# A planner of instruction order gets margins for the later expert searches, and ScalarE copies every expert's transposed tokens

## The chip, the core and the metric

The kernel runs on one core of a Trainium2 chip. TensorE (PE) multiplies matrices, VectorE (DVE), ScalarE (ACT) and GpSimd (POOL) work element by element, SyncE (SP) issues transfers, and DMA engines move data between the chip's memory and the core's two on-chip buffers, SBUF and PSUM; PE writes to PSUM only. The metric is the time of one execution on the device in microseconds (us), as the median of several runs; lower is better.

## The reference

Three parts follow one another: an attention whose keys and values are means over 8 rows, a mixture of experts in which each of 8 experts takes exactly as many tokens as its capacity, and a second MLP.

```python
scores = scale * np.matmul(q, k_p.transpose(0, 1, 3, 2))   # B=8, H=8, S=576, D=64; k_p, v_p pooled by 8
out    = softmax(scores) @ v_p                             # -> x: 4608 tokens x 512

logits = x @ w_gate                                        # 4608 x 8
cap    = N // E                                            # 576
order  = np.argsort(-logits.flatten())
for idx in order:                                          # the largest logits first
    tok, e = idx // E, idx % E
    if assigned[tok] >= 0 or counts[e] >= cap:
        continue
    assigned[tok] = e
    counts[e] += 1
for e in range(E):
    mask = assigned == e
    out[mask] = np.maximum(x[mask] @ w1[e], 0.0) @ w2[e]   # 512 -> 1024 -> 512

h = out @ w_in                                             # 512 -> 2048
y = (h - np.tanh(h)) @ w_out                               # 2048 -> 512
```

## The kernel before

After the attention the tokens' logits lie on chip and the tokens x in a buffer in the chip's memory (xd). `moe1` (L1190) then goes over the experts in the order in which they fill up. For step k it routes (`route`, L831, and `route_rows`, L920), writes down the work of the expert before (`expert(k - 1)`, L1140), and gathers the tokens of step k (`gather`, L1089).

A route finds the expert that fills next and the logit at which it is full. For k of 1 to 6 that is a search (`search`, L754) in steps: DVE compares logits with a row of thresholds (tile at), PE counts by 36 products with a one-hot matrix (rt<-at,ohb), DVE compares the counts with the places that are free (pass), PE spreads that over the partitions (rt<-pass,ones), and DVE picks the next thresholds. `fill` (L849) then marks the expert's tokens (sel), ranks them with a product on PE (`ahead`, L900: rt<-sel and rt<-run), makes their places (`slots`, L910) and takes the expert out of the logits. `route_rows` turns places into a list of row numbers: one-hot tables oa (DVE) and ob (DVE and POOL), 36 products of them (tr<-ob,oa), a cast (sp), five products (tr<-sp), and at last the numbers ix. `gather` fetches 5 tiles of token rows (xg) by an indirect transfer on POOL (L1098), transposes each with four PE instructions into the one PSUM tile of the name tr, and makes two parts of it: xh, a rounded copy (ACT), and xl, the rest (DVE). Every large matrix is held in two such parts, and a product of two matrices is three products of parts. All these parts are called "parts" in the trace. For expert 1 alone ACT first copies the PSUM tile over the row tile xg, which isn't needed any more, and both parts are taken from that copy.

`expert` does the first layer (8 tiles of 24 matmuls of 288 columns, into m and mm), splits its result in two (ACT, then DVE), and `outputs` (L1172) does the second. The weights come by SP's queue in tiles wr; ACT and DVE split them in two. Beside this, with low urgency, the weights of the second MLP are converted (tiles raw, ca, cd, cm, on DVE, ACT and POOL) and stored by SP's queue. `second_mlp` (L1236) begins when these and the first tiles of y, loaded by SP, are split.

The order of all this isn't the order of the code. `Plan` (L101) records every instruction with its reads and writes (so all of them carry line 129 in the profile), and `placed` (L228) takes the instructions whose inputs are placed by their urgency, the smaller number first, and puts each into the earliest gap on its engine. Between an instruction and one that uses its result it counts a fixed time (`latency`, L221). One unit of urgency is an eighth of an expert. Route k has 8k − 12.5, the gather 8k − 4.6, the first layer of expert k 8k to 8k + 3, its second 8k + 4 to 8k + 7. What comes out is a fixed order for each engine, in which an engine that waits for one instruction holds back all behind it.

Of the kernel before, what the change touches and what calls it, by code (L numbers as in the profile page):

```python
# [50 lines left out]
class Ring:  # L51


    def __init__(self, pool, banks=False):
        self.pool, self.banks, self.tiles, self.next = pool, banks, {}, {}
# [45 lines left out]
class Plan:  # L101
# [9 lines left out]
    def __init__(self, nc):  # L111
        self.nc = nc
        self.ops, self.seen = [], {}
        self.busy, self.done = {}, 0
        self.urgency = 0.0
        self.tensor, self.vector, self.scalar, self.gpsimd, self.sync = [
            Recorder(self, n) for n in ("tensor", "vector", "scalar", "gpsimd", "sync")]

# [47 lines left out]
    def call(self, engine, fn, ins, outs, cost, delay=0.0):  # L166

        op = self.Op()
        op.engine, op.fn, op.cost, op.delay, op.transfer = engine, fn, cost, delay, 0.0
        op.urgency, op.index, op.deps, op.users, op.end = self.urgency, len(self.ops), {}, [], None  # L170
        for aps, write in ((ins, False), (outs, True)):
            for ap in aps:
                name, lo, hi, p, q, dense = self.region(ap)
                log = self.seen.setdefault(name, [])
                keep = []
                for e in log:
                    o, w, lo2, hi2, p2, q2 = e
                    hit = lo < hi2 and lo2 < hi and p < q2 and p2 < q
                    if o is not op and hit and (write or w):
                        op.deps[o] = op.deps.get(o, False) or w  # L180
                    if not (write and dense and lo <= lo2 and hi2 <= hi and p <= p2 and q2 <= q):
                        keep.append(e)
                keep.append((op, write, lo, hi, p, q))
                self.seen[name] = keep
        for o in op.deps:
            o.users.append(op)
        self.ops.append(op)
        return op

    def after(self, op, other):  # L190
        if other not in op.deps:
            op.deps[other] = True
            other.users.append(op)
# [27 lines left out]
    def latency(self, op, user):  # L221
        if user.engine == op.engine and not op.transfer:
            return op.delay + (0.0 if op.engine == "tensor" or not user.deps[op] else 0.127)
        if user.engine == "tensor":
            return op.delay + (0.25 if op.engine == "scalar" else 0.22)
        return op.delay + (0.2 if op.engine == "tensor" or op.transfer else 0.14)

    def placed(self):  # L228
# [48 lines left out]
class Kernel:  # L277
# [571 lines left out]
    def fill(self, k, hl, t1, t2, ws, fl, after):  # L849

        c, rp, mw, L = self.c, self.rp, self.mw, self.L
        V = self.plan.vector
        more, at, gt = [rp.tile([128, NT], F32, name=nm) for nm in ("e1", "e2", "gt")]
        V.scalar_tensor_tensor(at, hl[:, 0], t1, mw, op0=OP.is_equal, op1=OP.mult)
        V.scalar_tensor_tensor(more, hl[:, 0], t1, mw, op0=OP.is_gt, op1=OP.mult)
        V.tensor_tensor(more, more, self.aid, op=OP.add)
        V.tensor_reduce(ws, fl, axis=AX.X, op=OP.max)
        V.scalar_tensor_tensor(gt, hl[:, 1], t2, at, op0=OP.is_gt, op1=OP.mult)
        V.scalar_tensor_tensor(at, hl[:, 1], t2, at, op0=OP.is_equal, op1=OP.mult)
        V.tensor_tensor(self.aid, more, gt, op=OP.add)  # L860
        sel = rp.tile([128, 2 * NT], BF, name="sel")
        V.tensor_scalar(sel[:, NT:], at, ws, None, op0=OP.is_equal)
        V.tensor_scalar(sel[:, :NT], self.aid, ws, None, op0=OP.is_equal)
        p1 = self.ahead(sel)
        val = rp.tile([128, 2 * NT], F32, name="val")
        V.scalar_tensor_tensor(val, p1, CAP - 0.5, sel, op0=OP.is_lt, op1=OP.mult)
        g = self.slots(k, p1, val)

        self.plan.urgency += 4.0
        cl = rp.tile([128, 8], F32, name="cl")  # L870
        V.tensor_scalar(cl, c["w8"], ws, -4.0e37, op0=OP.is_equal, op1=OP.mult)
        V.tensor_scalar(cl, cl, 1.0e37, None, op0=OP.add)
        ei = rp.tile([1, 1], I32, name=f"ei{k}")
        V.tensor_scalar(ei, ws[:1], -1.0, 8.0, op0=OP.mult, op1=OP.add)
        self.ei[k] = ei
        V.tensor_tensor(L, L, cl[:, None, :].to_broadcast([128, NT, 8]), op=OP.min)
        V.scalar_tensor_tensor(self.open, self.open, ws, self.open, op0=OP.not_equal, op1=OP.mult)
        after()
        if 0 < k < E - 2:
            self.best()  # L880
        V.scalar_tensor_tensor(self.aid, val[:, NT:], ws, self.aid, op0=OP.mult, op1=OP.add)
        self.plan.urgency -= 4.0
        return g

    def rest(self, live):
# [203 lines left out]
    def gather(self, k):  # L1089

        nc, P = self.nc, self.plan
        P.urgency = 8 * k - 4.6 if k else -12.5
        xh, xl = [self.fp.tile([128, 4, CAP], F32R, name=nm) for nm in ("xh", "xl")]
        rows = []
        for i in range(5):
            n = 64 if (k % 2 == 0 and i == 4) else 128
            xg = self.cv.tile([128, DM], F32, name="xg", bufs=5)
            op = P.call("gpsimd", lambda xg=xg, n=n, i=i: nc.gpsimd.indirect_dma_start(  # L1098
                out=xg[:n], out_offset=None, in_=self.xd,
                in_offset=bass.IndirectOffsetOnAxis(ap=self.idx[k][:n, i:i + 1], axis=0)),  # L1100
                [self.idx[k][:n, i:i + 1]], [xg[:n]], 1.3 if k == 0 else 1.04, 2.3 if k > 2 else 2.0)
            op.transfer = n * DM * 4 / 360e3
            self.gathered = op
            rows.append((xg, n))
        col = 0
        for i, (xg, n) in enumerate(rows):
            p0 = 64 if (k % 2 == 1 and i == 0) else 0
            if k or i % 3 == 0:
                pt = self.mps.tile([128, 4, 128], F32, name="tr")
            else:  # L1110
                pt = self.mps.tile([128, 2, 512], F32, name="mm", bufs=2)[:, 0].rearrange("p (d n) -> p d n", d=4)
            for d in range(4):
                P.tensor.transpose(pt[:, d, :n], xg[:n, d * 128:(d + 1) * 128], self.c["ident"][:n, :n])
            cs = slice(col, col + n - p0)
            if k == 1:

                xf = xg[:, :4 * n].rearrange("p (d n) -> p d n", d=4)
                P.scalar.activation(xf, pt[:, :, :n], AF.Copy)
                pt = xf
            P.scalar.activation(xh[:, :, cs], pt[:, :, p0:n], AF.Copy)  # L1120
            P.vector.tensor_tensor(xl[:, :, cs], pt[:, :, p0:n], xh[:, :, cs].bitcast(F32), op=OP.subtract)
            col += n - p0
        return xh, xl
# [66 lines left out]
    def moe1(self):  # L1190
        P = self.plan
        self.ei, self.ev, self.turns = {}, {}, 0
        for k in range(E):
            P.urgency = 8 * k - 12.5
            g = self.route(k)
            self.route_rows(k, g)
            if k:
                self.expert(k - 1)
            self.x = self.gather(k)
        self.expert(E - 1)  # L1200


# [256 lines left out]
```

## Time and profile before

| | us |
|---|---|
| median of 3 runs | 1507.74 |
| lowest and highest of them | 1506.91, 1509.02 |
| the profiled execution | 1509.08 |
| its span, from the first to the last instruction | 1507.3 |

The profiled execution lies 1.34 us above the median. In its span PE is busy 1445.5 us (96%), DVE 1194.8 (79%), ACT 796.2 (53%) and POOL 311.5 (21%). The attention ends and the first routing begins at about 148 us; the experts run from about 192 to 700 us, the second MLP until the end. A row of a timeline gives the start, the duration, the engine, the operation with what it writes and reads, and in brackets how long the engine had been idle and for what. A duration of "x24" is that of the whole row.

### The profile page before, as it was taken

The page shows a single profiled execution, that of the slowest core. Times are in us where ns is not written, and L with a number is a line of the kernel's source. Part 1 is how long each engine was busy: PE and PEld are TensorE (multiplying, and loading weights), DVE is VectorE, ACT ScalarE, POOL GpSimd, SP SyncE. Part 2 cuts the span into 40 slices and gives each one's busy share as a digit, 9 for nine tenths or more (in the row PEclk, how much of TensorE's full clock was granted, in tenths as well). Part 3 has the DMA queues.
Part 4 walks back from the last instruction along what each step waited for, and adds up shares of the span by engine and source line. Part 5 has one row for each costly group of instructions (what it writes and reads, how often), then busy time and mean ns, then how long its engine had stood idle before and what let it go on. Part 6 is the DMA issues. An engine that isn't in the chain of part 4 may idle for free.

```text
span 1507.3 us, 25587 instructions
## 1 busy us (share of the span) xinstructions
PE 1445.5 (96%) x9763; PEld 1272.5 (84%) x9764; DVE 1194.8 (79%) x2506; ACT 796.2 (53%) x1433; POOL 311.5 (21%) x292
## 2 busy tenths in 40 slices
PE   8999579999999998999999999999999999999997
PEld 7999368999998998999778888888888888888885
DVE  8777877767888887975998787877878787877874
ACT  5444114334463546884666565656556555565653
POOL 5873201102133225552411000010101001010101
PEclk9999689999999999999999999999999999999999
DMA  9942114424253456775201010000101000000000
GB/s 386 379 157 78 61 35 127 126 81 154 76 179 103 142 173 207 229 249 168 88 15 56 1 49 8 29 29 15 42 0 50 7 29 28 28 29 1 28 1 28
DMA packets 98315, 138.51 MB, mean 92 GB/s; under 512 B 6928, under 2 KB 70416, under 8 KB 95504
## 3 DMA queue, kind: packets, MB, share of 16 engines
q1 hardware_dynamic: 87632, 108.04, 21.1%
q0 software_dynamic: 5952, 19.40, 3.7%
q10 hardware_dynamic: 4608, 9.44, 1.6%
q8 instruction: 76, 1.25, 0.3%
q14 instruction: 47, 0.39, 0.1%
HBM read 103.30 MB, written 33.55 MB: 91 GB/s over the span
## 4 chain that ended last, share of the span: by engine, by line
PE 77%; DVE 16%; DMA 3%; issue 2%; ACT 1%; POOL 1%; SPq 0%; POOLq 0%; ACTq 0%; DVEq 0%
PE mm L129 36%; PE m L129 17%; PE tr L129 7%; PE rt L129 7%; PE av L129 4%; DVE parts L129 3%; PE sc L129 3%; PE pt L129 2%; DVE g L129 2%; DVE ca L129 2%; PE rt L659 1%; DVE oa L129 1%; DVE at L129 1%; DVE ob L129 1%; DMA wr<-w 1%
## 5 line engine op out<-in xcount | busy, mean ns | idle before, releaser
L129 PE MATMUL mm<-parts 128*128 128x288 f32 x2112 | 307.3, 300 | 3.8 <-DVE parts L129 3.8
L129 PEld LDWEIGHTS mm<-parts 128*128 128x128 f32 x2112 | 288.2, 190 | 7.1 <-DVE parts L129 3.9
L129 PE MATMUL mm<-parts,gh 128*128 128x512 f32 x792 | 243.9, 389 | 0.0
L129 DVE SCALAR_TENSOR_TENSOR g<-s,g 128x512 f32<-128x512 f32 x288 | 205.9, 715 | 2.8
L129 ACT ACTIVATE s<-u,pb 128x512 f32<-128x512 f32 x288 | 192.5, 724 | 0.0
L129 PEld LDWEIGHTS mm<-parts,gh 128*128 128x128 f32 x792 | 148.7, 188 | 30.9
L129 PE MATMUL mm<-parts,gl 128*128 128x512 f32 x396 | 154.4, 390 | 1.7 <-DVE gl L129 1.7
L1308 POOL DMA_INDIRECT out<-y,ix x18 | 20.1, 1116 | 657.8 <-ACT y L129 637.4
L129 PE MATMUL m<-parts 128*128 128x288 f32 x960 | 144.1, 301 | 0.0
L129 PE MATMUL m<-yh,parts 128*128 128x512 f32 x432 | 141.7, 389 | 0.0
L129 ACT ACTIVATE parts<-wr 128x512 fp32r<-128x512 f32 x148 | 90.5, 627 | 83.8 <-PE mm L129 47.2
L129 PEld LDWEIGHTS m<-parts 128*128 128x128 f32 x960 | 131.9, 189 | 2.3 <-issue 1.0
L129 ACT ACTIVATE gh<-g 128x512 fp32r<-128x512 f32 x144 | 91.2, 633 | 76.3 <-DVE g L129 54.2
L129 DVE TENSOR_TENSOR parts<-wr,parts 128x512 fp32r<-128x512 f32 x128 | 99.5, 789 | 30.0 <-ACT parts L129 28.8
L129 DVE TENSOR_TENSOR gl<-g,gh 128x512 fp32r<-128x512 f32 x144 | 105.2, 731 | 21.1 <-ACT gh L129 21.1
L129 DVE COPY_PREDICATED g<-m,t 128x512 f32<-128x512 uint32 x144 | 109.4, 760 | 5.0
L129 ACT ACTIVATE u<-m 128x512 f32<-128x512 f32 x72 | 42.8, 595 | 115.7 <-PE m L129 115.7
L129 PEld LDWEIGHTS m<-yh,parts 128*128 128x128 f32 x432 | 81.1, 188 | 16.9
L129 DVE TENSOR_TENSOR g<-m,u 128x512 f32<-128x512 f32 x72 | 49.4, 687 | 54.3 <-ACT t L129 53.3
L129 PEld LDWEIGHTS mm<-parts,gl 128*128 128x128 f32 x396 | 74.3, 188 | 18.2 <-DVE gl L129 3.0
L129 PE MATMUL m<-yl,parts 128*128 128x512 f32 x216 | 84.0, 389 | 0.0
L129 PE MATMUL tr<-yh,parts 128*128 128x512 f32 x216 | 70.9, 389 | 0.0
(273 smaller groups left out, 2847.0 us busy)
## 6 DMA issues: line engine op xcount, KB each, us to landing
wr<-w SPq DMA_DIRECT2D x64, 512.0 KB
xd<-x SPq DMA_DIRECT2D x36, 256.0 KB
yd<-y ACTq DMA_DIRECT2D x32, 288.0 KB
raw<-wi SPq DMA_DIRECT2D x32, 256.0 KB
raw<-wo SPq DMA_DIRECT2D x32, 256.0 KB
kr<-k SPq DMA_DIRECT2D x7, 1152.0 KB
qT<-q SPq DMA_DIRECT2D x7, 1152.0 KB
vr<-v SPq DMA_DIRECT2D x7, 1152.0 KB
```

What stands on the lines that cost most here:

```text
L129: op = self.call(engine, lambda: f(*args, **kw), ins, outs, cost, delay)
L659: last = self.nc.tensor.matmul(out, self.ohb[:, j, :], at[:, j, :], start=j == 0, stop=j == NT - 1)
L1308: st = nc.gpsimd.indirect_dma_start(out=self.io["out"], in_=o, in_offset=None, out_offset=bass.IndirectOffsetOnAxis(ap=at, axis=0))
```

## The change

Three things change.

First, the planner: an instruction on PE that is recorded while a margin is set counts that much more time between its inputs and itself. The margin is 0.8 us for the routes of experts 3 to 7, 0.2 for that of expert 2, and 1.5 for the gathers of experts 3 to 7. The routes of experts 2 to 7 become more urgent by 2.0, and the gathers of experts 3 to 7 by 0.9.

Second, `fill` of expert 1 raises its urgency number by 6.0 at its beginning, and this stays until the end of its list of rows, so that this end of the route has +1.5 in place of −4.5; the part of `fill` that had 4.0 more has 2.0 more now.

Third, in `gather` ACT copies the PSUM tile into xg for every expert but the first, and xh (ACT) and xl (DVE) are both taken from the copy.

```diff
@@ Plan.record, Plan.call, Plan.latency @@
         self.urgency = 0.0
+
+        self.margin = 0.0
...
         op.engine, op.fn, op.cost, op.delay, op.transfer = engine, fn, cost, delay, 0.0
+        op.margin = self.margin
...
         if user.engine == "tensor":
-            return op.delay + (0.25 if op.engine == "scalar" else 0.22)
+            return op.delay + (0.25 if op.engine == "scalar" else 0.22) + user.margin
@@ Kernel.fill @@
         more, at, gt = [rp.tile([128, NT], F32, name=nm) for nm in ("e1", "e2", "gt")]
+        if k == 1:
+
+            self.plan.urgency += 6.0
...
-        self.plan.urgency += 4.0
+        later = 2.0 if k == 1 else 4.0
+        self.plan.urgency += later
...
-        self.plan.urgency -= 4.0
+        self.plan.urgency -= later
@@ Kernel.gather @@
-        P.urgency = 8 * k - 4.6 if k else -12.5
+        P.urgency = 8 * k - (5.5 if k > 2 else 4.6) if k else -12.5
...
-            if k == 1:
+            if k:
 
                 xf = xg[:, :4 * n].rearrange("p (d n) -> p d n", d=4)
                 P.scalar.activation(xf, pt[:, :, :n], AF.Copy)
@@ Kernel.moe1 @@
-            P.urgency = 8 * k - 12.5
+            P.urgency = 8 * k - (14.5 if k > 1 else 12.5)
+            P.margin = 0.8 if k > 2 else 0.2 if k > 1 else 0.0
             g = self.route(k)
             self.route_rows(k, g)
+            P.margin = 0.0
             if k:
                 self.expert(k - 1)
+            P.margin = 1.5 if k > 2 else 0.0
             self.x = self.gather(k)
+            P.margin = 0.0
```

The code sets the order through the planner only. On PE, at the end of the routing of expert 1 (rt are the small products of the routing, m and mm the first-layer products of expert 0, oa and ob the one-hot tables), there stood before

```order
L129 MATMUL m_0_1670<-parts 128x288 x9
L129 MATMUL mm_1681<-parts 128x288 x4
L129 LDWEIGHTS ahead
L129 MATMUL rt_1641<-sel_1657,ahead 128x72
L129 LDWEIGHTS oneb
L129 MATMUL rt_1641<-run_1658,oneb 128x72
L129 LDWEIGHTS oa_1667
L129 MATMUL tr_1669<-ob_1668,oa_1667 40x32
```

and stands now

```order
L131 MATMUL m_0_1670<-parts 128x288 x9
L131 MATMUL mm_1681<-parts 128x288 x19
L131 LDWEIGHTS ahead
L131 MATMUL rt_1641<-sel_1657,ahead 128x72
L131 MATMUL mm_1681<-parts 128x288
L131 LDWEIGHTS oneb
L131 MATMUL rt_1641<-run_1658,oneb 128x72
L131 MATMUL mm_1681<-parts 128x288 x4
L131 MATMUL mm_1680<-parts 128x288 x24
L131 MATMUL m_0_1698<-parts 128x288 x2
L131 MATMUL m_0_1670<-parts 128x288 x2
L131 LDWEIGHTS oa_1667
```

Fifteen, one, and twenty-eight first-layer products stand now around the two products of the ranking, and four more ahead of the first product of the tables, so that these 48 come earlier than they did.

On DVE, at the same place (nm to ws are the last steps of the search, gt and e mark the tokens), there stood before

```order
L129 TENSOR_SCALAR t_0_1652<-nm_1651,t_1_1688 128x1
L129 SCALAR_TENSOR_TENSOR fl_1692<-rt_1641,nm_1651,w_144 128x8
L129 TENSOR_REDUCE ws_1653<-fl_1692 128x1
L129 SCALAR_TENSOR_TENSOR gt_1656<-hl_227,t_0_1652,e_0_1655 128x36
L129 SCALAR_TENSOR_TENSOR e_0_1655<-hl_227,t_0_1652,e_0_1655 128x36
L129 TENSOR_TENSOR aid<-e_0_1654,gt_1656 128x36
```

and stands now

```order
L131 TENSOR_SCALAR t_0_1652<-nm_1651,t_1_1688 128x1
L131 SCALAR_TENSOR_TENSOR fl_1692<-rt_1641,nm_1651,w_144 128x8
L131 TENSOR_TENSOR parts<-wr_1696,parts 128x512
L131 SCALAR_TENSOR_TENSOR parts<-mm_1680,parts 128x576
L131 SCALAR_TENSOR_TENSOR parts<-m_0_1698,parts 128x288
L131 SCALAR_TENSOR_TENSOR parts<-m_0_1670,parts 128x288
L131 TENSOR_REDUCE ws_1653<-fl_1692 128x1
L131 SCALAR_TENSOR_TENSOR gt_1656<-hl_227,t_0_1652,e_0_1655 128x36
L131 SCALAR_TENSOR_TENSOR e_0_1655<-hl_227,t_0_1652,e_0_1655 128x36
```

One part of a weight tile and the parts of three results of the first layer moved ahead of ws and of all that follows it.

On DVE, between the last table oa and the cast sp, there stood before

```order
L129 TENSOR_SCALAR ob_1668<-ob_1668,pcol 128x192
L129 TENSOR_TENSOR oa_1667<-gb_1666,iota_151 128x480
L129 TENSOR_TENSOR logits<-logits,cl_1662 128x288
L129 SCALAR_TENSOR_TENSOR open<-open,ws_1653 128x8
L129 SCALAR_TENSOR_TENSOR yc_0_1694<-thr,nm_1651,z_0_1691 8x42
L129 TENSOR_REDUCE most_1642<-yc_0_1694 8x1
L129 TENSOR_TENSOR lack<-lack,most_1642 8x1
L129 TENSOR_SCALAR full_1664<-w8c,ws_1653 8x1
L129 CAST sp<-tr_1669 40x32
```

and stands now

```order
L131 TENSOR_SCALAR ob_1668<-ob_1668,pcol 128x192
L131 TENSOR_TENSOR oa_1667<-gb_1666,iota_151 128x480
L131 TENSOR_TENSOR parts<-wr_1697,parts 128x512 x2
L131 CAST sp<-tr_1669 40x32
L131 TENSOR_TENSOR logits<-logits,cl_1662 128x288
L131 SCALAR_TENSOR_TENSOR open<-open,ws_1653 128x8
L131 TENSOR_TENSOR wi_1671<-tr_1669,pick 128x160
```

Two parts of weights moved in between; a row of small steps moved behind sp.

On PE, in the search of route 4 (pass is the outcome of the count before, the row after the last is the first of the 36 products of the next count), there stood before

```order
L129 MATMUL m_0_1698<-parts 128x288 x2
L129 MATMUL m_0_1670<-parts 128x288 x2
L129 LDWEIGHTS ones
L129 MATMUL rt_1641<-pass_162,ones 128x41
L129 MATMUL m_0_1670<-parts 128x288 x16
L129 MATMUL m_0_1698<-parts 128x288
```

and stands now

```order
L131 MATMUL mm_1680<-parts 128x288 x10
L131 LDWEIGHTS ones
L131 MATMUL rt_1641<-pass_162,ones 128x41
L131 MATMUL mm_1680<-parts 128x288 x5
L131 MATMUL tr_1669<-ident,xg_1675 128x128 x4
L131 MATMUL m_0_1698<-parts 128x288 x12
L131 MATMUL m_0_1670<-parts 128x288 x3
```

Between the product with pass and the next count there were 17 matmuls, and are 20 and four transposes of the gather.

On ACT, at the gather of expert 7 (cm, cd and raw belong to the conversion for the second MLP), there stood before

```order
L129 ACTIVATE parts<-wr_1696 128x512
L129 ACTIVATE parts<-mm_1681 128x576
L129 ACTIVATE parts<-tr_1669 128x4x64
L129 ACTIVATE parts<-wr_1696 128x512
L129 ACTIVATE cm_1721<-cm_1721 128x512
L129 ACTIVATE cd_1718<-raw_1713 128x512
L129 ACTIVATE parts<-tr_1669 128x4x128
```

and stands now

```order
L131 ACTIVATE xg_1675<-tr_1669 128x512
L131 ACTIVATE parts<-wr_1697 128x512
L131 ACTIVATE parts<-m_0_1698 128x288
L131 ACTIVATE cm_1720<-cm_1720,cmin 128x512
L131 ACTIVATE xg_1676<-tr_1669 128x512
L131 ACTIVATE parts<-m_0_1670 128x288
L131 ACTIVATE cm_1720<-cm_1720 128x512
L131 ACTIVATE cd_1719<-raw_1714 128x512
L131 ACTIVATE cm_1721<-raw_1714 128x512
L131 ACTIVATE xg_1677<-tr_1669 128x512
L131 ACTIVATE parts<-wr_1696 128x512
L131 ACTIVATE parts<-xg_1675 128x4x64
```

The copies xg<-tr are new; the parts xh follow behind them, read xg, and no longer read tr.

## Rows read from the trace of the kernel before

**Rows 1.** Stretches: length, busy us (x instructions) of five engines, granted clock, DMA share.

```profile
215.00:229.00 14.00, 4.50 (x58) 3.82 (x57) 13.37 (x53) 0.41 (x1) 3.79 (x5) 0.73 0.06 14
...
435.00:502.00 67.00, 62.66 (x661) 59.91 (x660) 58.00 (x147) 31.47 (x60) 19.35 (x17) 1.00 0.40 132
...
sum 1507.00, PE 1445.45 PEld 1272.52 DVE 1194.77 ACT 796.17 POOL 311.49; mean PE 96.36 PEld 84.83 DVE 79.65 ACT 53.08 POOL 20.77
```

**Rows 2.** PE's waits, 192 to 242 us: waited for, total us, times, longest.

```profile
PE tr L129 <- DVE oa L129: 4.9, 3, 3.0
PE mm L129 <- DVE parts L129: 3.8, 1, 3.8
```

**Rows 3.** PE's waits, 242 to 700 us.

```profile
PE tr L129 <- DVE parts L129: 8.2, 6, 2.9
PE rt L659 <- DVE at L129: 2.2, 3, 0.9
PE tr L129 <- DVE sp L129: 1.2, 5, 0.2
PE rt L129 <- DVE run L129: 1.0, 1, 1.0
PE rt L129 <- ACT z L129: 0.8, 3, 0.3
PE rt L129 <- DVE ei L129: 0.4, 1, 0.4
```

**Rows 4.** Timeline of PE: start us, duration us, operation [idle before].

```profile
228.39 7.55 PE L129 MATMUL mm<-parts 128*128 128x288 f32 x44 [3.77 <-DVE parts L129]
235.78 3.34 PE L129 MATMUL m<-parts 128*128 128x288 f32 x24
238.97 3.34 PE L129 MATMUL mm<-parts 128*128 128x288 f32 x24
```

**Rows 5.** Timeline of DVE, end of the routing of expert 1.

```profile
222.01 0.96 DVE L129 TENSOR_TENSOR oa<-gb,iota 128x480 bf16<-128x480 bf16 x1
...
227.65 1.28 DVE L129 TENSOR_TENSOR parts<-wr,parts 128x512 fp32r<-128x512 f32 x2
...
229.53 0.81 DVE L129 SCALAR_TENSOR_TENSOR parts<-m,parts 128x288 fp32r<-128x288 f32 x2
```

**Rows 6.** Timeline of POOL, gather 1; chain of waits, gather 0.

```profile
226.48 1.01 POOL L1098 DMA_INDIRECT xg<-xd,ix  x1 [4.02 <-issue]
...
187.19 4.35 DMA xg<-xd,ix
```

**Rows 7.** Timelines of PE and of DVE, gather of expert 6.

```profile
573.42 1.12 PE L129 MATMUL tr<-ident,xg 128*128 128x128 f32 x4 [2.90 <-DVE parts L129]
574.19 2.83 PE L129 MATMUL mm<-parts 128*128 128x288 f32 x12
...
572.69 0.68 DVE L129 TENSOR_TENSOR parts<-tr,parts 128x512 fp32r<-128x512 f32 x1
```

**Rows 8.** Tile xg, 242 to 260 us: ns min/median/max, first and last start.

```profile
L129 ACT ACTIVATE xg<-tr x5: 592/601/601, 242.9 to 248.3; 128x512 f32<-128x512 f32 x5
```

**Rows 9.** Tiles tr, wr on DVE; groups, 380 to 700: busy, mean.

```profile
L129 DVE TENSOR_TENSOR parts<-tr,parts x30: 402/691/693, 307.6 to 641.3; 128x512 fp32r<-128x512 f32 x24, 128x256 fp32r<-128x256 f32 x6
...
L129 DVE TENSOR_TENSOR parts<-wr,parts x80: 669/684/1761, 369.7 to 682.0; 128x512 fp32r<-128x512 f32 x80
...
L129 DVE TENSOR_TENSOR parts<-wr,parts 128x512 fp32r<-128x512 f32 x81 | 67.9, 847 | 18.4 <-ACT parts L129 17.3 <-issue 1.0
```

**Rows 10.** Timeline of PE, search of route 4.

```profile
386.75 1.07 PE L659 MATMUL rt<-at,ohb 128*8 128x41 bf16 x36 [0.69 <-DVE at L129]
```

**Rows 11.** The second MLP's start: POOL's timeline, tile yh, PE's timeline.

```profile
680.95 1.62 POOL L129 TENSOR_TENSOR cm<-cm,ca 128x512 f32<-128x512 f32 x1
...
L129 DVE TENSOR_TENSOR yl<-yr,yh x4: 684/686/692, 689.5 to 691.3; 128x512 fp32r<-128x512 f32 x4
...
697.08 0.40 PE L129 MATMUL rt<-yh,uh 128*128 128x512 f32 x1
```

## The prediction, made before the changed kernel had run

> **What bounds the kernel now.** I read the busy time by stretch first. TensorE (PE) is busy 1445.45 of 1507.00 us, VectorE (DVE) 1194.77, ScalarE (ACT) 796.17: PE is the bound, and a change gains only where PE stands. One stretch stands out: from 215 to 229 us PE works 4.50 of 14.00 us while DVE works 13.37 [rows 1]. The list of PE's waits in 192 to 242 us names what PE stood for there: 4.9 us for DVE's one-hot tables oa, the longest 3.0, and 3.8 for DVE's weight parts [rows 2]. It is the end of the routing of expert 1: its rows are ranked (sel, run), turned into lists (oa, ob, sp, ix) and gathered, and PE has nothing between. The same list for 242 to 700 us holds 13.8 us in small pieces: 8.2 us, in 6 places, where a transpose of gathered tokens (tr) waits for DVE's parts; 4.4 us in the searches (at 2.2, run 1.0, z 0.8, ei 0.4); and 1.2 on sp [rows 3]. So about 23 us of idle time lie where the change works.
>
> **The hole at 215 us (fill of expert 1 made less urgent).** In the changed order 51 of expert 0's matmuls move: 48 of them ahead of the 36 products tr<-ob,oa, 3 ahead of the five that read sp. 24 such matmuls start at 235.78 and the next 24 at 238.97, so one takes 3.19/24 = 0.133 us, and 51 take 6.8. Before, 44 of them ran after the hole from 228.39 to 235.78, 7.39 us where 44 × 0.133 = 5.9 would do: the granted clock was 0.73 in the hole and had yet to rise [rows 1, 4]. If nothing waited any more, the hole would give its 9.5 us of idle time and 1.5 of slow matmuls, 11.0.
>
> DVE holds some of that back, since it now makes expert 0's parts ahead of the ranking: one parts<-wr, one parts<-mm, two parts<-m. In the trace a pair of parts<-wr and a parts<-mm take from 227.65 to 229.53 and two parts<-m 0.81; less one parts<-wr (half of 1.28) that is 1.88 − 0.64 + 0.81 = 2.1 us. The third oa ended at 222.01 + 0.96 = 222.97 and ends at 225.1 now [rows 5]. PE, with 48 more matmuls (6.4 us) behind 216.6, arrives at the products at 223.2; two blocks of them of about 0.5 bring it to 224.2, and it waits 0.9 for the third oa. Between that oa and sp two more parts<-wr (1.28) now stand on DVE, so sp comes at 226.6 and PE, after its three matmuls, waits 0.7. The gather of expert 1 comes later too: its first transfer started at 226.48, now at 228.6; a transfer of the gather before landed 4.35 us after its start, so the first row is there at 232.95 [rows 6]. PE needs it at 242.14 (the end of the second 24) less 11.0 − 0.9 − 0.7 = 9.4, at 232.7. Rows land 1.3 us apart, the pace of the transposes with their six matmuls, and I allow 0.8 us of waits. I take 9.4 − 0.8 = **8.6 us**. Bounds: 11.0 if DVE and the transfers keep nobody waiting; 5 if the 3.8 on weight parts stays whole.
>
> **Copies of the transposed tokens (30 new ACT instructions).** Until now, from expert 2 on, ACT made xh and DVE made xl straight from PSUM, and the one PSUM tile came free with the later of the two. The longest wait shows the price: at 573.42 PE had stood 2.90 us, since DVE, behind other parts, came to parts<-tr at 572.69 only [rows 7]. Expert 1's five tiles already run the new way; their copies take 601 ns [rows 8]. With a copy, the tile is free one ACT instruction after its transposes, and the transposes stand some 1.6 us apart (12 matmuls). ACT is busy 796 of 1507 us, so its queue is mostly short. I take all **8.2 us** as gone; if in two of the six places ACT is two instructions late, 2 × 1.2 = 2.4 stay. The 2.90 us had a second price: the 12 matmuls behind it took 2.83 us where 12 take 1.6, **1.2 us** [rows 4, 7]. The copies cost ACT 27 × 0.60 and three half as wide 3 × 0.4, 17.4 us, all beside PE's matmuls; without that cover it would be the whole 17.4.
>
> DVE's part changes too: xl then has both inputs in SBUF, where one was in PSUM. parts<-tr took at most 693 ns in 30 instances; parts<-wr, which has two SBUF inputs already, has a median of 684 and a longest of 1761 ns in 80, and a mean of 847 in 380 to 700 us, where POOL works too [rows 9]. So the 24 wide xl of experts 2 to 7 may cost 24 × (0.847 − 0.691) = 3.7 us of DVE time. DVE is busy 58.00 of 67 us in 435 to 502 [rows 1], so the cover is thin, and I put it all on PE's path: **−3.7 us**. Bounds: 0, and 24 × (1.761 − 0.691) = 25.7.
>
> The Trainium skill has a rule on this, on the page "SBUF — State Buffer", section "Who interferes with whom": a VectorE instruction with two SBUF inputs contends with a GpSimd instruction that reads SBUF, one with at most one SBUF input (outside the two-port modes) does not, and the one issued first holds the shared ports for its whole instruction. The trace agrees: 693 ns at most against up to 1761. The rule speaks against this part of the change; rival A is what it would do here.
>
> **Margins of the searches (experts 2 and later).** A step of a search goes from DVE to PE and back, and PE's order was planned with a fixed time for the way. Where DVE was later, PE stood, as 0.69 us at 386.75 ahead of the 36 products of route 4 [rows 10]. Between pass and those products the order now has 20 matmuls and four transposes for 17 matmuls: 3 × 0.133 + 0.45 = 0.85 us more. That covers the waits on at (0.9 at most), z (0.3) and ei (0.4); run (1.0, once) keeps about 0.2 by it, which the same route's earlier start may take. So **4.4 us**; bounds 2.2 (at only) and 5.6 (sp too). The 1.2 on sp I count unchanged. A search gets some 6 × 0.8 = 5 us longer, but starts 2 units of urgency earlier (a unit is an eighth of an expert, about 8 us), so nobody waits for its end.
>
> **What stays.** The second MLP's matmuls keep their order. Its start could be hit: POOL's last conversion ended at 680.95 + 1.62 = 682.6, and SP, whose queue is in order, loads y behind the store of it. yl was ready at 691.3 + 0.69 = 692.0, and PE's first product with y ran at 697.08 without a wait: 5.1 us of slack [rows 11].
>
> **Sum.** 8.6 + 8.2 + 1.2 + 4.4 − 3.7 = 18.7 us. The profiled execution took 1509.08 us, so 1490.4; it lies 1.34 above the median, 1507.74, so **1489** in the median, 1.2% less.
>
> **Rivals.** *A: DVE's lag comes back.* xl, slowed by POOL, delays all that is queued behind it on DVE: at, pass, parts. The 13.8 us of waits in 242 to 700 stay in size under other names, and the hole and the clock remain: 1509.08 − 8.6 − 1.2 = 1499.3, 1498 in the median (1494 to 1503). For it: the 1761 ns and DVE's 87%. Against: the mean is 847, and xl is not needed at once. *B: all idle time goes*: 11.0 + 13.8 + 1.2 = 26.0, 1482. Against: DVE worked 13.37 of 14 us in the hole. *C: nothing is gained.* The parts are DVE's work wherever they stand, and if the 51 matmuls find theirs no earlier than before, the hole only moves; with A's lag the time is about 1506. Against: the change puts just those parts first. *D: slower.* The conversions for the second MLP share ACT and DVE with the last two gathers. If their ten copies (0.6 each) and ten xl (1.07 more each) push POOL's last conversion back by 16.7 us, yl comes 16.7 − 5.1 = 11.6 us too late; with nothing gained, as in C, that is 1506 + 11.6 = 1518. It decides once POOL's last cm ends after 687.7 us. Against: it takes every xl at its slowest.
>
> **How the numbers follow.** Forecast 0.60 (its own range 1484 to 1495), A 0.22, B 0.06, C 0.06, D 0.06. Predicted is the forecast's time. From 1482, B's time, to 1501 lie the forecast, most of A and half of B, a little over 8 in 10. A measurement of this kernel can tell about 0.2% (3 us) from no change. Forecast, A and B are faster by more, 0.88; C is the same, 0.06; D slower, 0.06.
>
> **What the profile after would show.** In 215 to 229 us PE busy over 10 us at a granted clock above 0.73; expert 0's last products end near 233. PE's waits of tr on DVE parts are gone, with none above 0.5 us on ACT in their place. ACT's busy time is up by 17 us. xl has a mean near 0.85 us with few above 1.5. Waits on at are below 0.5 us in all. I am wrong if xl's mean is above 1.2, if PE's waits on DVE in 242 to 700 stay above 10 us, if PE stands over 2 us for the gather's DMA near 233, or if it waits for yl near 690.

## The result, and the profile of the changed kernel

The changed kernel took 1487.73 us in the median of 4 runs (1486.26 to 1488.65), against 1508.36 for the kernel before, run beside it. The ratio is 0.9861 (0.9846 to 0.9877), some 21 us less. The profiled execution has a span of 1485.9 us.

To see where the time went I cut both spans at the same three events: the product rt<-dl that ends the search of expert 1, the first transposes of gather 1, and the first product with y. A row gives the stretch, its length, the busy time of PE, of its weight loads, of DVE, ACT and POOL, the granted clock, the DMA share and the GB/s moved. Before:

```profile
214.68:242.14 27.46, 17.96 (x151) 17.28 (x150) 22.92 (x68) 5.57 (x11) 6.89 (x8) 0.81 0.35 107
242.14:697.08 454.94, 440.78 (x4294) 426.18 (x4293) 363.38 (x878) 235.58 (x428) 135.22 (x112) 1.00 0.48 155
697.08:1507.30 810.22, 797.57 (x3554) 660.87 (x3552) 641.29 (x1040) 472.16 (x812) 68.67 (x56) 1.00 0.09 29
```

After:

```profile
214.12:231.25 17.13, 16.12 (x152) 15.49 (x151) 16.31 (x53) 5.05 (x10) 4.38 (x6) 1.00 0.27 80
231.25:677.31 446.06, 439.30 (x4294) 426.36 (x4293) 364.36 (x892) 249.92 (x461) 145.10 (x115) 0.99 0.50 160
677.31:1485.90 808.59, 797.01 (x3554) 661.18 (x3552) 641.92 (x1041) 471.50 (x811) 68.69 (x56) 1.00 0.09 30
```

The hole gave 27.46 − 17.13 = 10.3 us, the experts behind it 8.9, the second MLP 1.6, and 0.6 came from ahead of the first event. The granted clock in the first stretch is 1.00 where it was 0.81. In the experts PE's idle time fell from 14.2 to 6.8 us; the busy time of PE fell by 1.5.

This is the timeline of PE in what was the hole, for [rows 4] (line 129 of the kernel before is line 131 of the changed one, and 659 is 662):

```profile
215.43 2.67 PE L131 MATMUL mm<-parts 128*128 128x288 f32 x19
...
218.26 3.96 PE L131 MATMUL mm<-parts 128*128 128x288 f32 x28
...
224.30 0.47 PE L131 MATMUL tr<-ob,oa 128*40 128x32 bf16 x12 [0.84 <-DVE oa L131]
...
228.07 3.34 PE L131 MATMUL mm<-parts 128*128 128x288 f32 x24
231.25 0.60 PE L131 MATMUL tr<-ident,xg 128*128 128x128 f32 x4
...
234.13 0.63 PE L131 MATMUL tr<-ident,xg 128*128 128x128 f32 x4 [1.35 <-DMA xg<-xd,ix]
```

Of the waits of [rows 2] only 0.84 us on oa is left, and a new one of 1.35 on the gather's second row of tokens. For [rows 3], PE's waits from 231 to 700 us are now these (what it waited for, total, times, longest):

```profile
PE tr L131 <- DVE sp L131: 2.4, 2, 2.3
PE mm L131 <- DVE parts L131: 2.0, 1, 2.0
PE tr L131 <- DMA xg<-xd,ix: 1.4, 1, 1.4
PE rt L131 <- DVE pass L131: 0.8, 1, 0.8
```

All six waits of transposes on DVE parts are gone, and so are those on at, run, z and ei. Two new ones of 2.3 and 2.0 us have come.

### The profile page after: what moved, and what is told of

Read it like the earlier page. It is cut to its first block, busy times and chain, and to the rows that moved or that the text cites. A ratio compares the mean times of both kernels' runs of the same rounds, so it can differ in the third digit from the quotient of the medians.

```text
span 1485.9 us, 25650 instructions
## 1 busy us (share of the span) xinstructions
PE 1441.4 (97%) x9763; PEld 1271.1 (86%) x9764; DVE 1190.2 (80%) x2506; ACT 809.2 (54%) x1463; POOL 318.2 (21%) x292
## 4 chain that ended last, share of the span: by engine, by line
PE 85%; DVE 9%; issue 2%; DMA 2%; ACT 1%; POOL 1%; POOLq 0%; ACTq 0%; DVEq 0%; SPq 0%
PE mm L131 40%; PE m L131 19%; PE tr L131 8%; PE rt L131 7%; PE av L131 4%; PE sc L131 3%; PE pt L131 2%; DVE parts L131 2%; PE rt L662 2%; DVE g L131 2%; DVE ca L131 1%; DVE gl L131 1%; DMA xg<-xd,ix 1%; DVE oa L131 1%; DVE ob L131 0%
```

## The experiments

I undid the parts one by one, made them one by one, and then paired them. The kernel before ran beside each; the gain is (1 − ratio) × 1508 us. The interval of a ratio is about ±0.0016, some 2.5 us.

| kernel | median, us | ratio to before (95%) | gain, us |
|---|---|---|---|
| changed kernel | 1487.73 | 0.9861 (0.9846 to 0.9877) | 21.0 |
| fill alone | 1502.60 | 0.9954 (0.9938 to 0.9971) | 6.9 |
| copies alone | 1511.02 | 1.0007 (0.9997 to 1.0016) | −1.1 |
| all margins and urgencies alone | 1505.28 | 0.9978 (0.9964 to 0.9992) | 3.3 |
| all but the copies | 1498.08 | 0.9923 (0.9906 to 0.9939) | 11.6 |
| all but the fill | 1496.88 | 0.9920 (0.9904 to 0.9937) | 12.1 |
| copies and gather margin | 1499.19 | 0.9938 (0.9922 to 0.9955) | 9.3 |
| all but the gather margin | 1495.97 | 0.9924 (0.9901 to 0.9946) | 11.5 |
| all but the route margins | 1489.70 | 0.9867 (0.9851 to 0.9883) | 20.1 |
| all, xl from PSUM | 1491.12 | 0.9888 (0.9870 to 0.9906) | 16.9 |
| all, two margins more | 1484.66 | 0.9833 (0.9814 to 0.9853) | 25.2 |

What a part is worth "in the whole" is the gain that is lost when it alone is taken from the changed kernel; such worths don't add up where parts depend on each other.

### The fill alone

```diff
         more, at, gt = [rp.tile([128, NT], F32, name=nm) for nm in ("e1", "e2", "gt")]
+        if k == 1:
+            self.plan.urgency += 6.0
...
-        self.plan.urgency += 4.0
+        later = 2.0 if k == 1 else 4.0
+        self.plan.urgency += later
```

> Only the lower urgency of expert 1's fill is changed against the kernel before. Theory (each part does its own work): the hole at 215 us shrinks as it did in the changed kernel, where the stretch from the product with dl to the first transposes of gather 1 fell from 27.4 to 17.1 us and one wait of 1.4 us on the gather's DMA came up; so 9 to 10 us less than before, about 1499, and in 242 to 700 us the old waits stay (tr on DVE parts about 8, at about 2). Rival (the parts need each other: the matmuls that fill the hole are missing later): under 5 us less, with new waits on DVE parts between 230 and 300 us.

Measured: 6.9 us less than before. From rt<-dl to the first transposes it took 233.73 − 215.07 = 18.7 us, 8.8 less than before, and then the gather's DMA kept PE waiting for 0.44 us. The stretch behind it, to the first product with y, took 457.5 us where it took 454.9. The waits in 242 to 700 us stayed, 8.4 us of them on tr:

```profile
PE tr L131 <- DVE parts L131: 8.4, 6, 2.8
```

So the hole closes by the fill alone, somewhat less than expected, and the part closes nothing else.

### The copies alone

```diff
-            if k == 1:
+            if k:
 
                 xf = xg[:, :4 * n].rearrange("p (d n) -> p d n", d=4)
```

> Only the copies of the transposed tokens are added to the kernel before, for every expert but the first; the planner is unchanged. Theory: the six waits of tr on DVE parts (8.2 us) and the slow matmuls behind the longest (1.2) go, the lengthened two-input xl cost 2 to 4 us: 5 to 7 us less than before, about 1502; waits on at and run stay at 2 to 5 us. Rival (it was the margin of 1.5 us, not the copy, that removed the waits of tr): waits of tr remain above 4 us, now on ACT xg, and the time is within 3 us of before.

Measured: no gain, 1.0007. The theory fell. The six waits on DVE parts are gone, but in 242 to 700 us PE waits for other things instead, 12.6 us where it waited 13.8; the largest are (dl is a small tile at the end of a search, made by DVE; yh is the first part of y, made by ACT for the second MLP):

```profile
PE rt L131 <- DVE dl L131: 2.6, 3, 0.9
PE tr L131 <- ACT xg L131: 2.4, 3, 1.5
PE tr L131 <- DVE oa L131: 2.3, 1, 2.3
PE tr L131 <- DVE sp L131: 1.9, 6, 0.7
PE rt L131 <- ACT yh L131: 1.8, 1, 1.8
```

The timelines of PE and of ACT at the gather of expert 6 show the longest wait for a copy, the tile xg:

```profile
572.21 0.66 PE L131 MATMUL tr<-ident,xg 128*128 128x128 f32 x4 [1.48 <-ACT xg L131]
572.62 1.04 PE L131 MATMUL mm<-parts 128*128 128x288 f32 x6
573.55 0.66 PE L131 MATMUL tr<-ident,xg 128*128 128x128 f32 x4
```

```profile
569.89 0.72 ACT L131 ACTIVATE cm<-cm,cmin 128x512 f32<-128x512 f32 x1
570.52 0.61 ACT L131 ACTIVATE parts<-wr 128x512 fp32r<-128x512 f32 x1
571.04 0.63 ACT L131 ACTIVATE parts<-mm 128x576 fp32r<-128x576 f32 x1
571.57 0.58 ACT L131 ACTIVATE xg<-tr 128x512 f32<-128x512 f32 x1
```

The planner, which counts a copy as quick, sets the transposes 6 or 7 matmuls apart, 1.34 us from the second to the third. The copy is quick, 0.58 us, but it stands on ACT behind three other instructions that ran late, and PE stood 1.48 us. The wait for the tile went from DVE's queue to ACT's. That is 2.4 of the 12.6 us.

More than half of the rest stands behind DVE instructions that ran beside POOL's work. xl itself was hardly slower here, a mean of 703 ns, but other DVE instructions with two inputs in SBUF were. Ahead of each of the three waits on dl a parts<-wr, 0.68 us when nothing is in its way, took 1.75 us while POOL ran cm<-cm,ca. From the timelines of POOL, DVE and PE at the first of them:

```profile
396.98 2.64 POOL L131 TENSOR_TENSOR cm<-cm,ca 128x512 f32<-128x512 f32 x1
...
398.42 1.75 DVE L131 TENSOR_TENSOR parts<-wr,parts 128x512 fp32r<-128x512 f32 x1
...
401.49 0.18 PE L131 MATMUL rt<-dl,ones 128*128 128x8 f16 x1 [0.88 <-DVE dl L131]
```

The wait on oa stands behind one table of 1.75 us, where the two before it took 0.64, and the 0.7 on sp behind a parts<-wr of 1.75:

```profile
580.22 1.26 POOL L131 TENSOR_TENSOR cm<-cm,ca 128x512 f32<-128x512 f32 x1
...
580.24 1.75 DVE L131 TENSOR_TENSOR oa<-gb,iota 128x480 bf16<-128x480 bf16 x1
```

So 5.6 us of the new waits (dl 2.6, oa 2.3, sp 0.7) stand behind DVE instructions that took over 1 us longer beside POOL. The kernel before has such pairs too, at other places: the 0.69 us of [rows 10] stands behind an at that took 2.71 us, where one a little narrower, with no POOL work beside it, took 1.71:

```profile
383.98 2.71 DVE L129 SCALAR_TENSOR_TENSOR at<-hl,t,thr 128x1476 bf16<-128x1476 f32 x1
...
385.22 2.60 POOL L129 TENSOR_TENSOR cm<-cm,ca 128x512 f32<-128x512 f32 x1
```

No run moved or removed POOL's work, so this is read from the traces and not shown by an experiment.

### The margins alone

```diff
-        P.urgency = 8 * k - 4.6 if k else -12.5
+        P.urgency = 8 * k - (5.5 if k > 2 else 4.6) if k else -12.5
...
-            P.urgency = 8 * k - 12.5
+            P.urgency = 8 * k - (14.5 if k > 1 else 12.5)
+            P.margin = 0.8 if k > 2 else 0.2 if k > 1 else 0.0
...
+            P.margin = 1.5 if k > 2 else 0.0
             self.x = self.gather(k)
```

> Only the margins and the four urgencies of the later routes and gathers are changed against the kernel before; no copies, and the fill of expert 1 as before. Theory: the search waits (at, run, z, ei, 4.4 us) go, the waits of tr on DVE parts stay at 5 us or more: 3 to 5 us less than before, about 1504; the hole at 215 us stays at 9.5 us idle. Rival (the margins also cure the waits of tr, since the gather's 1.5 us keeps its transposes apart): tr waits below 2 us and 10 us or more less, about 1497.

Measured: 3.3 us less, in the theory's range. The waits on at, run and z are gone (0.9 on inc, beside at in the same search step, is new), those on ei rose from 0.4 to 1.9 against the theory, and those of tr stayed:

```profile
PE tr L131 <- DVE parts L131: 10.2, 6, 4.9
PE rt L131 <- DVE ei L131: 1.9, 2, 1.2
```

### All but the copies

```diff
-            if k:
+            if k == 1:
```

> The changed kernel with copies for expert 1 alone, as it was before. Theory: tr waits on DVE parts come back, 4 to 8 us, and the two-input cost goes: 1492 to 1496, 4 to 8 us slower than the changed kernel. Rival (margins cure the waits of tr): within 2 us of the changed kernel's 1487.7, with tr waits below 2 us.

Measured: 0.9923, so the copies are worth 21.0 − 11.6 = 9.4 us where the margins and the fill are there, more than the theory had. The waits of tr are back:

```profile
PE tr L131 <- DVE parts L131: 9.9, 6, 4.4
```

The margins without copies don't cure them, and the copies alone bring nothing. So the next runs pair the copies with the gather's margin alone, or take one partner from the whole.

### Copies and the gather margin; all but the gather margin

The first adds to the copies the 1.5 us of margin and the urgency of the gathers; the second is the changed kernel without them.

```diff
+            P.margin = 1.5 if k > 2 else 0.0
             self.x = self.gather(k)
...
-        P.urgency = 8 * k - 4.6 if k else -12.5
+        P.urgency = 8 * k - (5.5 if k > 2 else 4.6) if k else -12.5
```

> The kernel before with the copies, the gather margin of 1.5 us and the gather's urgency; routes as before, without margin. With the copies alone the waits were 2.4 on ACT xg (the transposes had moved closer, 6 matmuls apart), 2.6 on dl, 1.1 on pass, 2.3 on oa, 1.9 on sp. Theory (the gather margin cures what hangs on the gather's own tile, the route margin what hangs on the searches): xg below 0.5, the others about the same or 1 less: 3 to 5 us under the copies alone, about 1506. Rival (the gather margin is the whole interplay): 10 us under the copies alone, about 1500.

> The changed kernel without the gather margin and with the gather's old urgency; copies, route margins and the fill stay. Theory (as in the run with the gather margin alone): waits of tr on ACT xg of 2 to 3 us come back with the slower matmuls behind them, 3 to 5 us slower than the changed kernel: about 1492. Rival (the route margin does nothing, the gather margin all): 8 to 10 us slower, about 1497.

Measured: 9.3 us of gain where the copies alone lost 1.1, and 21.0 − 11.5 = 9.5 us of loss when the gather margin is taken from the whole. By price the rival won in both: the copies' partner is the gather's margin together with the urgency that goes with it. No run takes these two apart. With both, no transpose waits for ACT. In the changed kernel's timeline of PE the transposes of gather 6 stand 18 matmuls apart, 2.83 us:

```profile
548.38 0.60 PE L131 MATMUL tr<-ident,xg 128*128 128x128 f32 x4
548.73 2.64 PE L131 MATMUL mm<-parts 128*128 128x288 f32 x18
551.21 0.60 PE L131 MATMUL tr<-ident,xg 128*128 128x128 f32 x4
```

A copy that comes 1.5 us late finds its time there. But the waits on xg in the copies alone were 2.4 us, and some 10 were won; the rest went at other places. The waits on dl show how: with the gather's margin and urgency POOL ran nothing beside the parts<-wr ahead of the first of them, which took 0.68 us, and no wait on dl is left. The planner set the whole neighbourhood anew, and that some of POOL's work fell elsewhere isn't what the margin was meant for. How much of the 10 us is distance and how much is this, no run separates.

Without the gather margin two waits on the copy return, and the start of the second MLP is late:

```profile
PE rt L131 <- ACT yh L131: 3.8, 1, 3.8
PE tr L131 <- ACT xg L131: 2.6, 2, 2.1
```

Against the changed kernel's span of 1485.9 us this one's is 1492.9. The longer wait on xg, 2.06 us, came behind 2.39 us in which ACT, ahead of that copy, stood for POOL's cm. PE's idle time is 3.5 us longer, since these 6.4 us and some 1.4 of small waits stand against the 4.3 that only the changed kernel has, and PE's busy time is 3.5 us longer (1444.9 against 1441.4), which I didn't follow place by place.

### All but the fill; all but the route margins

The first is the changed kernel with expert 1's fill as before, the second the one with this in place of the routes' two lines:

```diff
-            P.urgency = 8 * k - (14.5 if k > 1 else 12.5)
-            P.margin = 0.8 if k > 2 else 0.2 if k > 1 else 0.0
+            P.urgency = 8 * k - 12.5
```

> The changed kernel with expert 1's fill as urgent as before: copies, margins and urgencies stay. From the first product with dl to the first product with y it took 482.4 us before, 463.2 in the changed kernel, 476.1 with the fill alone, 483.2 with the copies alone and 479.3 with the margins alone. Theory now (copies and margins need each other, the fill stands by itself): 463.2 + 6.3 = 469.5 us for that stretch, about 1494 in all, with the hole's 9.5 us idle back and waits of tr below 3 us in 242 to 700. Rival (the fill is what lets the copies work): 476 us or more, about 1501, the waits of tr or of the searches above 6 us.

> The changed kernel without the margins of the routes and with their old urgency; the fill, the copies and the gather margin stay. Copies and gather margin alone gave 9.9 us, the fill alone 7.0. Theory (the fill adds up with the rest, and the copies pair with the gather margin): 1509 - 9.9 - 7.0 to 9 = about 1491, 3 us slower than the changed kernel, with waits on at of 2 to 3 us and on sp of 1.2 back. Rival (the route margins are a partner of the copies too): 1495 or more, with waits above 8 us in 242 to 700.

Measured: without the fill 0.9920, a loss of 8.9 us, and from rt<-dl to the first product with y 470.6 us, where 469.5 were expected; the fill stands by itself. Without the route margins 0.9867, a loss of 0.9 us, which can't be told from none. The waits that they are for did come back:

```profile
PE rt L662 <- DVE at L131: 2.9, 4, 1.1
PE tr L131 <- DVE sp L131: 1.1, 5, 0.2
PE tr L131 <- DVE oa L131: 1.0, 1, 1.0
```

But this kernel hasn't the 2.3 us on sp in one place, and only 0.8 of the 2.0 on parts, which the changed one has at 662.91. The route margins took some 5 us of small waits away and brought nearly as much back in fewer, larger ones.

### xl from PSUM

ACT copies, xh is made from the copy, but xl from the PSUM tile.

```diff
+            ps = pt
             if k:
...
-            P.vector.tensor_tensor(xl[:, :, cs], pt[:, :, p0:n], xh[:, :, cs].bitcast(F32), op=OP.subtract)
+            P.vector.tensor_tensor(xl[:, :, cs], ps[:, :, p0:n], xh[:, :, cs].bitcast(F32), op=OP.subtract)
```

> The changed kernel, in which ACT makes the copy and xh is taken from it, but xl is taken from the PSUM tile again, so that it has one input in SBUF and the tile comes free only after xl. Theory (two inputs in SBUF are what lengthens xl, and the early release of the tile is what the copy is for): the longest wide xl falls from 1.78 to 0.70 us, and the waits of tr on DVE parts come back at 5 us or more, as without copies (9.9): 1495 to 1500. Rival (the waits went because xl, and not the tile, was in the way): waits of tr below 2 us and a time of 1485 to 1488, since xl is shorter.

Measured: the longest xl is 693 ns. The first row is the changed kernel's tile xg from 258 us on, the second this kernel's tile tr; a row gives minimum, median and maximum in ns:

```profile
L131 DVE TENSOR_TENSOR parts<-xg,parts x30: 403/680/1781, 306.4 to 616.2; 128x512 fp32r<-128x512 f32 x24, 128x256 fp32r<-128x256 f32 x6
```

```profile
L131 DVE TENSOR_TENSOR parts<-tr,parts x35: 410/679/693, 233.2 to 630.1; 128x512 fp32r<-128x512 f32 x28, 128x256 fp32r<-128x256 f32 x7
```

The second input in SBUF is thus what lengthens xl. The waits of tr on DVE parts came back, 5.3 us (3.9 of them on transposes), and the ratio is 0.9888, 4 us worse than the changed kernel; the two intervals overlap a little, so this is near the limit of what can be told. That is 4 us better than the theory's 1495 and 3 worse than the rival's 1488: the waits returned, as the theory had it, but the changed kernel's waits of 2.3 us on sp and 2.0 on parts are gone, which I hadn't counted. The early release of the tile is what took the waits of tr away.

### Two margins more

```diff
-            P.margin = 0.8 if k > 2 else 0.2 if k > 1 else 0.0
+            P.margin = 2.0 if k == E - 1 else 0.8 if k > 2 else 0.2 if k > 1 else 0.0
...
-            P.margin = 1.5 if k > 2 else 0.0
+            P.margin = 1.5 if k > 2 else 1.0 if k == 1 else 0.0
             self.x = self.gather(k)
```

> The changed kernel with two more margins, against the largest waits that are left: 1.0 us for the gather of expert 1 (its transposes waited 1.4 us on the gather's DMA), and 2.0 in place of 0.8 for the route of expert 7 (its sp was 2.3 us late behind lengthened xl). Theory (a margin that covers a measured wait removes it): 2 to 4 us less than the changed kernel, about 1485, both waits below 0.5. Rival (the longer routes and gathers shift the rest, and new waits of this size come): within 2 us of it.

Measured: 1484.66 us, 0.9833 (0.9814 to 0.9853), some 4 us less than the changed kernel, whose interval overlaps with this one's. The wait of 1.4 us on the gather's DMA is gone, as the theory had it. The wait on sp is still 2.0 us, at 562.90, so a margin doesn't always remove the wait that it was set for. What also went is the wait of 2.0 us on parts at 662.91 of the changed kernel, with the slow matmuls behind it, at which neither margin was aimed; waits of 0.8 us on yh and 0.5 on xg came. So time and theory agree, but half of the theory fell.

## Why the prediction held, point by point

The forecast was 1489 and the time is 1487.73. Its sum was 18.7 us, and 21.4 were won between the two spans. By place it held too: 8.6 us forecast and 9.0 measured in the hole, 10.1 and 10.2 in the experts behind it (the 1.35 us on the gather's DMA counted in the hole), and 2.2 in places that I hadn't foreseen. The mechanism held for the hole and in part for the rest. Term by term:

**The hole: right, in place and size.** Forecast 8.6; the stretch gave 10.3, less the 1.35 on the gather's DMA 9.0, and taking the fill away costs 8.9. The wait for the third oa was forecast at 0.9 and is 0.84, sp kept nobody waiting where I had 0.7, and the transfers cost 1.35 where I allowed 0.8. The 24 matmuls ahead of the gather end at 231.25; I had 232.7, on a clock of events that began 0.6 later. Rival C fell by this.

**The transposes: the waits went, but the step that says why was wrong.** I wrote that with a copy the transposes stand "some 1.6 us apart (12 matmuls)" and gave all 8.2 us, and 1.2 for the clock, to the copies. In gather 6 they stand 2.83 us and 18 matmuls apart with the gather's margin and urgency, and 1.34 us and 6 matmuls without them: the distance is the work of a part of the change that the prediction doesn't cost at all. The copies alone gain nothing; with the gather margin they gain 9.3. The bound that I gave for a late ACT, 2.4 us, is just what the copies alone show on ACT xg. What I had missed is that a new order also sets anew which DVE instructions run beside POOL's; the waits on dl, oa and sp of that run stand behind such ones. My reading of the longest wait of the kernel before stopped too early as well: DVE was behind "other parts" at 572.69 [rows 7] since a parts<-wr from 570.20 took 1.76 us beside POOL's ca<-ca,cd.

**xl: right in kind, nearly in size.** The 24 wide ones of experts 2 to 7 have a mean of 784 ns, so 24 × (0.784 − 0.688) = 2.3 us more than parts<-tr had, where I had 3.7, which set a mean against a median. The six narrow ones, which I hadn't counted, took 586 instead of 416 ns, 1.0 more: 3.3 in all. The group rows of the changed kernel (busy us, mean ns):

```profile
L131 DVE TENSOR_TENSOR parts<-xg,parts 128x512 fp32r<-128x512 f32 x24 | 18.8, 784 | 0.6 <-ACT parts L131 0.6
L131 DVE TENSOR_TENSOR parts<-xg,parts 128x256 fp32r<-128x256 f32 x6 | 3.5, 586 | 0.7 <-ACT parts L131 0.7
```

The trace shows at one place how this reaches PE. POOL ran cm<-cm,ca from 554.67 for 1.43 us and from 558.08 for 1.32; in both stretches a DVE instruction with two SBUF inputs took over 1 us longer than elsewhere, sp came late behind them, and PE stood 2.27 us until 560.90:

```profile
554.88 1.78 DVE L131 TENSOR_TENSOR parts<-xg,parts 128x512 fp32r<-128x512 f32 x1
...
557.99 1.56 DVE L131 SCALAR_TENSOR_TENSOR ca<-raw,ca 128x128 int32<-128x128 int32 x2
...
560.67 0.17 DVE L131 CAST sp<-tr 40x32 bf16<-40x32 f32 x1
```

The wait of 2.01 us until 662.91 stands behind such a pair too, here with the weight parts, which had two SBUF inputs before the change as well; two of them take 1.3 us elsewhere:

```profile
659.82 2.36 DVE L131 TENSOR_TENSOR parts<-wr,parts 128x512 fp32r<-128x512 f32 x2
...
660.04 1.59 POOL L131 TENSOR_TENSOR ca<-ca,cd 128x512 int32<-128x512 int32 x1 [0.29 <-DVE ca L131]
```

This is rival A's mechanism at two places: 4.3 us of waits, and 1.7 of slower matmuls behind the second, where A had all of the 13.8 us of waits stay. The rule of the Trainium skill, "SBUF — State Buffer", section "Who interferes with whom", is borne out by the run with xl from PSUM: with one SBUF input 693 ns at most in 35, with two up to 1781 in 30.

**The searches: the waits went, the gain was mis-sized.** Of at, run, z and ei, 4.4 us, nothing is left; yet the route margins are worth 0.9 us in the whole and can't be told from nothing. The step that failed is to count a removed wait as a gain: without the margins 5.0 us of small waits are there, with them 4.3 us of large ones.

**Rival D was nearer than I had it.** Its price hung on 5.1 us of slack ahead of the second MLP. In the changed kernel yl is ready at 676.0 + 0.69 = 676.7 and PE's first product with y runs at 677.31: 0.6 is left. With the copies alone POOL's last cm ended at 686.86 + 1.29 = 688.15, past the 687.7 that I had named, and PE waited 1.8 us for yh; without the gather margin 3.8. The price was small since nothing like 16.7 us of ACT and DVE work came to stand in the way. One reason isn't the conversion: ACT, in order, was idle 9.19 us for a weight tile whose transfer SP issued behind y's, and made yh only after it (y's own transfer had waited on SP for the store of the last conversion):

```profile
671.42 1.15 ACT L131 ACTIVATE parts<-wr 128x512 fp32r<-128x512 f32 x2 [9.19 <-DMA wr<-w]
...
673.51 2.20 ACT L131 ACTIVATE yh<-yr 128x512 fp32r<-128x512 f32 x4 [0.40 <-ACT y L131]
```

**Not foreseen**: 1.6 us in the second MLP (the waits on gl fell from 1.9 to 0.8) and 0.6 ahead of the hole; and the wait of 2.0 us on parts with slower matmuls behind it.

Of the signs that I had named, PE was busy 12.99 of the 14 us from 215 to 229 at a granted clock of 1.00, and xl's mean stayed below 0.85 us; ACT's busy time rose by 13.0 us, not by 17.

So the total came out right in part by luck. What the copies and the margins of the searches are worth in the whole I had wrong, and the errors (copies 5.7 us where 9.4 are lost without them, searches 4.4 where 0.9 are) nearly cancel. Only the hole is right in mechanism and size.

## What to carry to other kernels

In a schedule that is fixed beforehand, a buffer that comes free sooner can gain nothing, since the planner moves its next use closer and sets all that stands around it anew. Here the copies paid only where the planner also counted more time for the release. So cost a quicker release and the distance to the next use together, look at both in the order and not at the duration of the copy, and look at what now runs beside what: the waits that came with a new order stood for the most part behind DVE instructions with two SBUF inputs beside POOL's work. A wait that goes isn't a gain until the new ones are counted. A stretch in which the bounding engine has nothing queued (here 9.5 us in one hole) was the safest term of this sum: work that was ready could be moved in, for 6.9 us alone and 8.9 in the whole.

## What the runs showed of the hardware

At two places of the changed kernel a wait of 2 us was paid again in part by slower matmuls. 48 of them that take 6.52 us elsewhere took 8.19 behind the wait of 2.01 us; the granted clock was 0.79 in that stretch, a mean of its two levels of 1.2 and 2.4 GHz, and 1.00 ahead of the wait and behind the stretch:

```profile
662.91 8.19 PE L131 MATMUL mm<-parts 128*128 128x288 f32 x48 [2.01 <-DVE parts L131]
...
680.08 6.52 PE L131 MATMUL mm<-parts 128*128 128x288 f32 x48
```

Behind the 2.27 us on sp the clock was 0.68 for 5.3 us. Without the fill the same 48 matmuls took 8.18 us behind a wait of 1.97. But with the fill alone the clock was 0.76 from 226.6 to 233.7 us, and from 193 us to there PE had no wait above 0.85; the changed kernel, with the same order there and a wait of 0.84, stayed at 1.00. Why, no run shows.

The transfers of the gathers mostly took longer than the 4.35 us that I had from one row: from issue to landing 3.3, 6.0 and 8.2 us (least, median, most) for the changed kernel's gathers.
